# First weight pieces, softmax maxima and reciprocals in PSUM, and v_m products on half rows

## The chip, the cores and the metric

The kernel runs on one core of a Trainium2 chip. The metric is the device time of one execution in microseconds; the median of the runs counts. Engines are named as in the profile: PE is TensorE (matmul), PEld its weight loads, DVE VectorE, ACT ScalarE, POOL GpSimd, SP SyncE (its queue issues the DMAs).

## The reference

Three stages follow one another, all in float32. First a linear attention with 32 memory slots for 8 batches and 8 heads of 576 positions and 64 features; then two feed-forward stages over the 4608 rows of 512 features.

```python
a = softmax(phi, axis=2)                          # over the 576 positions, (8, 8, 576, 32)
k_m = einsum('bhsm,bhsd->bhmd', a, k)             # (8, 8, 32, 64)
v_m = einsum('bhsm,bhsd->bhmd', a, v)
attn = softmax(q @ k_m.T / sqrt(64), axis=-1)     # over the 32 slots
x = attn @ v_m                                    # -> (4608, 512)
h = x @ w_in                                      # (512, 2048)
x = maximum(0.01 * h, h) @ w_out                  # (2048, 512)
out = (sigmoid(x @ w_gate) * (x @ w_val)) @ w2_out
```

The weights arrive in float64, so each element of a weight is two 32-bit words.

## The kernel before, in words

**Precision.** Weights are read as pairs of words and turned into float32 by integer operations (class Piece), and each matrix is then split into a high and a low part (split: a copy on ScalarE, a subtraction on VectorE or GpSimd), so that one product becomes three matmuls.

**Pieces.** The weights of the first feed-forward stage are 32 pieces of 128 x 512 elements, four for each block j of 256 columns of w_in: pieces 4j and 4j+1 are w_in, 4j+2 and 4j+3 rows of w_out. A piece passes five stages: a (three ScalarE passes, L214, L215 and L222: y, k and the sign), b (VectorE, L226, clamps y), b2 (VectorE, L234, shifts y and sets the sign), c (GpSimd, L242, adds k), d (w_out only: the split, at L186 and L187). One call of tick() moves five pieces on by one stage each. The buffers are y (five) and k (four); k comes free when c has run.

**Units.** A unit is one batch and four of its heads. Its parts have names: v1, t1, v2, t2, v3, v3e, v4 are the first softmax (its maximum over positions needs a transpose t1 and a product t2 on TensorE), t4 builds k_m and v_m, v5r and v5x scale them, t5 and v6 transpose them into kvT, t8 and v8 give the scores, v9m, v9s, v9e, v10r, v10m the second softmax, v10t and v11 transpose and split the result. t parts are TensorE's, v parts are others'; upool lists those that GpSimd does.

**Folding v_m into w_in.** Since x = attn @ v_m, the kernel computes vw = v_m @ w_in per batch (vw_block for batch 0, vw_pair for two blocks of a later batch) and then h = attn @ vw in m1_in. For batch 0 kvT holds v_m with zeros in the other half's rows, and vw_block multiplies all 128 rows; vw_pair uses 64 rows for each of the two groups of heads, in two PSUM banks.

**PSUM.** There are eight banks: ps_acc has four (sums of m1_out), ps_h two (m1_in), ps_a two (everything else: t1, t2, t4, t5, t8 and the vw products).

**Order.** All is written out by hand. The prologue computes units 0 and 1 in groups of parts from SCHED; within a group the chains of all units, of the ticks (T) and of a waiting vw split take turns, each up to its next yield. Then 256 steps (batch, half, fc) follow. Step i, in emission order: the split of step i+1's m1_in (gh on ScalarE; gl on GpSimd, or on VectorE for the steps in gldve), then m1_in of step i+2 (six matmuls; gr on ScalarE), the v parts of this step with the held split of the last vw block and the ticks, the t parts, a vw block if the step is in vw0, and m1_out of step i (twelve matmuls). Every engine runs its instructions in this order. A unit's parts stand at fixed distances from its first step (chain1 for batch 1; its units begin at steps 1 and 13). Batch 0's sums are closed after every four steps and copied or added to SBUF (L844 on ScalarE, L842 on VectorE). The second feed-forward stage (m2_group, m2_out) comes after all steps.

## Time and profile before

| | us |
|---|---|
| median of 3 runs | 1602.17 (1600.76 to 8618.76) |
| the profiled execution | 1601.75 |
| its span | 1599.90 |
| TensorE busy in the span | 1549.1 (97%) |
| VectorE busy | 827.7 (52%) |
| ScalarE busy | 707.9 (44%) |
| GpSimd busy | 431.0 (27%) |

The span is the time from the first to the last instruction; the profiled execution's own time lies 1.85 us above it. The page's granted clock is in shares of TensorE's full clock of 2.4 GHz; 0.50 is the lower level of 1.2 GHz. It is at full over the whole span but for the first 80 us and a few short stretches. Most of batch 0 lies between 50 and 160 us, and before 50 us there is the prologue.

### The profile page before, as it was taken

The page shows a single profiled execution, that of the slowest core. Times are in us where ns is not written, and L with a number is a line of the kernel's source. Part 1 is how long each engine was busy: PE and PEld are TensorE (multiplying, and loading weights), DVE is VectorE, ACT ScalarE, POOL GpSimd, SP SyncE. Part 2 cuts the span into 40 slices and gives each one's busy share as a digit, 9 for nine tenths or more (in the row PEclk, how much of TensorE's full clock was granted, in tenths as well). Part 3 has the DMA queues.
Part 4 walks back from the last instruction along what each step waited for, and adds up shares of the span by engine and source line. Part 5 has one row for each costly group of instructions (what it writes and reads, how often), then busy time and mean ns, then how long its engine had stood idle before and what let it go on. Part 6 is the DMA issues. An engine that isn't in the chain of part 4 may idle for free.

```text
span 1599.9 us, 27447 instructions
## 1 busy us (share of the span) xinstructions
PE 1549.1 (97%) x10544; PEld 1358.0 (85%) x10544; DVE 827.7 (52%) x1426; ACT 707.9 (44%) x1602; POOL 431.0 (27%) x429
## 2 busy tenths in 40 slices
PE   5799999999999999999999999999999999999998
PEld 2677988999999998999988888888888888888898
DVE  6886444555554545422145474355545475255544
ACT  5885455565556555645333143223333143223332
POOL 3886343554445444543100020000200020000100
PEclk8799999999999999999999999999999999999999
DMA  9822554554556455322446446536546446536692
GB/s 306 277 53 64 160 143 138 150 154 139 159 146 192 140 160 146 115 82 97 146 170 218 140 156 234 191 115 222 195 163 222 141 150 236 169 109 223 223 398 76
DMA packets 203490, 268.66 MB, mean 168 GB/s; under 512 B 95072, under 2 KB 140128, under 8 KB 203360
## 3 DMA queue, kind: packets, MB, share of 16 engines
q1 hardware_dynamic: 203360, 266.92, 52.1%
q8 instruction: 83, 1.36, 0.4%
q14 instruction: 47, 0.39, 0.1%
HBM read 219.68 MB, written 47.19 MB: 167 GB/s over the span
## 4 chain that ended last, share of the span: by engine, by line
PE 82%; ACT 1%; DVE 1%; DMA 1%; issue 0%; POOL 0%; DVEq 0%; SPq 0%; ACTq 0%; POOLq 0%
PE acc L835 20%; PE oacc L1041 18%; PE ps_y L943 14%; PE ps_h L813 9%; PE ps_x L943 9%; PE ps_z L943 9%; PE ps_vw L783 1%; PE ps_kv L550 1%; DMA wt<-gvs 1%; PE ps_sc L625 0%; ACT gr L818 0%; ACT obuf L844 0%; DVE vw L795 0%; DVE t L530 0%; ACT raw L222 0%
## 5 line engine op out<-in xcount | busy, mean ns | idle before, releaser
L835 PE MATMUL acc<-gh,wo 128*128 128x288 f32 x2048 | 428.7, 301 | 3.7 <-ACT obuf L844 2.7
L835 PEld LDWEIGHTS acc<-gh,wo 128*128 128x128 f32 x2048 | 328.9, 189 | 28.4 <-issue 13.8
L835 PE MATMUL acc<-gl,wo 128*128 128x288 f32 x1024 | 304.8, 298 | 2.1 <-POOL gl L187 2.1
L187 POOL TENSOR_TENSOR gl<-gr,gh 128x288 fp32r<-128x288 f32 x250 | 215.6, 864 | 329.9 <-ACT gh L186 216.6
L1041 PE MATMUL oacc<-w2t,pt 128*128 128x512 f32 x1296 | 296.3, 389 | 0.0
L1041 PEld LDWEIGHTS oacc<-w2t,pt 128*128 128x128 f32 x1296 | 243.1, 188 | 50.3
L943 PE MATMUL ps_y<-xo,wt 128*128 128x512 f32 (+1 forms) x1080 | 251.9, 369 | 0.0
L813 PE MATMUL ps_h<-at_hi,vw 128*128 128x288 f32 x1024 | 214.6, 298 | 6.1 <-ACT vw L186 4.7
L943 PEld LDWEIGHTS ps_y<-xo,wt 128*128 128x128 f32 x1080 | 190.4, 188 | 33.8
L818 ACT ACTIVATE gr<-ps_h 128x288 f32<-128x288 f32 x256 | 105.7, 413 | 254.2 <-PE ps_h L813 226.1
L906 POOL TENSOR_TENSOR xo<-xr,xo 128x512 fp32r<-128x512 f32 (+1 forms) x16 | 23.0, 1460 | 671.0 <-ACT xo L902 671.0
L835 PEld LDWEIGHTS acc<-gl,wo 128*128 128x128 f32 x1024 | 193.7, 189 | 3.0 <-POOL gl L187 3.0
L813 PEld LDWEIGHTS ps_h<-at_hi,vw 128*128 128x128 f32 x1024 | 166.6, 190 | 7.5 <-ACT vw L186 5.6
L943 PE MATMUL ps_z<-xo,wt 128*128 128x512 f32 (+1 forms) x720 | 167.4, 368 | 0.6 <-DMA wt<-gvs 0.6
L943 PE MATMUL ps_x<-xo,wt 128*128 128x512 f32 (+1 forms) x720 | 167.5, 368 | 0.0
L813 PE MATMUL ps_h<-at_lo,vw 128*128 128x288 f32 x512 | 151.6, 296 | 0.0
L978 ACT CAST pt<-sg 128x512 fp32r<-128x512 f32 (+1 forms) x120 | 69.4, 578 | 182.0 <-DVE sg L971 182.0
L943 PEld LDWEIGHTS ps_z<-xo,wt 128*128 128x128 f32 x720 | 127.0, 189 | 23.1 <-DVE tmp L1024 0.7
L943 PEld LDWEIGHTS ps_x<-xo,wt 128*128 128x128 f32 x720 | 127.2, 188 | 22.9
L186 ACT CAST gh<-gr 128x288 fp32r<-128x288 f32 x256 | 111.8, 437 | 2.2
L813 PEld LDWEIGHTS ps_h<-at_lo,vw 128*128 128x128 f32 x512 | 97.2, 190 | 0.0
L990 ACT COPY tmp<-ps_x 128x512 f32<-128x512 f32 (+1 forms) x60 | 32.5, 542 | 136.6 <-PE ps_x L943 136.6
(171 smaller groups left out, 1719.0 us busy)
## 6 DMA issues: line engine op xcount, KB each, us to landing
wt<-gvs SPq DMA_DIRECT2D x210, 512.0 KB, 4.6
w2t<-w2s SPq DMA_DIRECT2D x60, 512.0 KB, 5.5
gvs<-hl SPq DMA_DIRECT2D x84, 256.0 KB, 2.4
x2s<-obuf SPq DMA_DIRECT2D x15, 576.0 KB, 3.7
win<-in_moe_w_in_dram SPq DMA_DIRECT2D x16, 512.0 KB, 9.8
wo_bits<-in_moe_w_out_dram SPq DMA_DIRECT2D x16, 512.0 KB, 10.4
xr<-x2s SPq DMA_DIRECT2D x16, 512.0 KB, 6.2
out_dram<-osum SPq DMA_DIRECT2D x32, 256.0 KB, 2.0
```

What stands on the lines that cost most here:

```text
L186: nc.scalar.copy(hi, raw)
L187: eng.tensor_sub(lo, raw, f32(hi))
L550: nc.tensor.matmul(p[M * h:M * h + M, 0:2 * D], a, x, start=(c == 0), stop=(c == CC))
L783: nc.tensor.matmul(ps[g][M * h:M * h + M, n * VB:(n + 1) * VB], kvT[b, g][D * g:D * g + D, 1, M * h:M * h + M], win[j][D * g:D * g + D, h, ...
L813: nc.tensor.matmul(p[:, :HALF], w, x, start=(n == 0), stop=(n == 3 * NG - 1))
L818: nc.scalar.activation(gr, p[:, :HALF], AF.Prelu, alpha=0.01)
L835: nc.tensor.matmul(a[d][:, :HALF], w[:, ds_], x, start=(open_ and n == 0), stop=(close and n == 2),)
L906: eng.tensor_sub(t[:, 1, :h], x_operand(n, k, a), f32(t[:, 0, :h]))
L943: nc.tensor.matmul(bank, w[:, l, a, :], x[:, r, :h], start=(start and i == 0), stop=(i == 5), skip_group_check=not start,)
L978: nc.scalar.copy(d[:, 0, :h], s)
L990: read(lambda: nc.scalar.copy(s1, x))
L1041: nc.tensor.matmul(bank[i], pt[2 * f + t][:, l, q * P:(q + 1) * P], w2t[f][:, r, :], start=(f == 0 and l + r == 0), stop=(f == TH - 1 and ...
```

## The change

Five things are changed, with the schedule numbers that belong to them:

- The first nine pieces (banks: 9) get their y in a bank of ps_acc from stage a on; b clamps it there, and b2 reads it from there and writes its result to an SBUF y tile.
- In batch 0 the tile st of the second softmax (maximum, sum, reciprocal) lies in a bank of ps_h. GpSimd has no part in v9s and v10m of batch 0 any longer (upool), so VectorE does both.
- The product of the mask and the reciprocal in v5r (VectorE, L565) becomes an activation on ScalarE in v5x, into a tile of its own.
- vw_block makes its products on 64 rows for each group, as vw_pair does, and so takes two tiles of ps_a where it took one; its split is two copies of 256 columns and two subtractions, with a yield between. Blocks 0 and 1 are computed together at the end of the last but one prologue group (W), and their split takes turns with that of the last group.
- v1 of the first unit of batch 1 leaves the prologue. In chain1 v1, t1, v2 and t2 stand at -1, 0, 1 and 2 in place of -5, -1, 0 and 1; block 5 of batch 0 is made at step 12 in place of 13.

```diff
--- before.py
+++ after.py
@@ -18,16 +18,17 @@
 
 
 
-SCHED = {'vw0': [2, 5, 8, 13, 20, 22],
+SCHED = {'vw0': [2, 5, 8, 12, 20, 22],
  'loads': ['p0', 'q0', 'k0', 1, 'p1', 1, 'k1', 'q1', 2, 'p2', 16, 'k2', 32, 'q2.0', 'q2.1', 'q2.2', 'q2.3'],
  'prologue': ['v1.0', 't1.0', 'v2.0 t7a.0 t2.0', 'v7a.0 v3.0', 'v3e.0 v4.0', 't7b.0 v1.1', 'T t4.0 t1.1', 'T',
               'v5.0', 'v7b.0', 'v2.1', 't5.0', 'v6.0 t2.1 t8a.0', 'T v3.1', 'v3e.1 v8a.0 t8b.0', 't7a.1', 'v8b.0',
-              'v9.0 v7a.1 T v4.1 v9e.0 t4.1', 't7b.1 T', 't5.1 v5.1 v7b.1', 'T v1.2', 'v10.0 T', 't8a.1 v6.1',
-              'v10t.0 t8b.1 T v8a.1', 'v11.0', 'v8b.1 v9.1 T', 'T T v9e.1 T v10.1 v10t.1 v11.1'],
+              'v9.0 v7a.1 T v4.1 v9e.0 t4.1', 't7b.1 T', 't5.1 v5.1 v7b.1', 'T', 'v10.0 T', 't8a.1 v6.1',
+              'v10t.0 t8b.1 T v8a.1', 'v11.0', 'v8b.1 v9.1 T', 'T T v9e.1 W', 'T v10.1 v10t.1 v11.1'],
  'ticks': [1, 1, 1, 1, 2, 1, 1, 2, 0, 1, 0, 1, 1, 2, 0, 0, 0, 1, 1, 1, 1, 1, 0, 0, 1, 0, 0, 0, 0, 0],
+ 'banks': 9,
  'lopool': [0, 1, 2, 3, 4, 5, 6, 7, 8, 9, 10, 11, 12, 13, 14],
  'gldve': [3, 4, 6, 12, 26, 31],
- 'upool': ['v10.1', 'v10.2', 'v10.3', 'v11.0', 'v11.1', 'v11.2', 'v11.3', 'v9.0', 'v9.2', 'v9.3'],
+ 'upool': ['v10.2', 'v10.3', 'v11.0', 'v11.1', 'v11.2', 'v11.3', 'v9.2', 'v9.3'],
  'chain': {'lp': -8,
            'lk': -5,
            'lq0': -8,
@@ -94,10 +95,10 @@
             'lq1': 0,
             'lq2': 1,
             'lq3': 2,
-            'v1': -5,
-            't1': -1,
-            'v2': 0,
-            't2': 1,
+            'v1': -1,
+            't1': 0,
+            'v2': 1,
+            't2': 2,
             'v3': 3,
             'v3e': 3,
             'v4': 4,
@@ -195,7 +196,7 @@
     PC = 512
 
     class Piece:
-        late = False
+        late = bank = False
 
         def __init__(self, src, done, f_dst=None, raw=None):
             self.src, self.done, self.f_dst, self.raw = src, done, f_dst, raw
@@ -209,7 +210,10 @@
 
         def a(self):
             w = self.raw.rearrange("p (n t) -> p n t", t=2)
-            self.y = cvp.tile([P, PC], F32, tag="y", name="y", bufs=5)
+            if self.bank:
+                self.y = ps_acc.tile([P, PC], F32, tag="acc", name="y_bank")
+            else:
+                self.y = cvp.tile([P, PC], F32, tag="y", name="y", bufs=5)
             self.k = cvp.tile([P, PC], F32, tag="k", name="k", bufs=4)
             nc.scalar.activation(self.y, w[:, :, 1].bitcast(F32), AF.Abs, scale=2.0 ** -3)
             nc.scalar.activation(self.k, w[:, :, 0], AF.Copy, scale=2.0 ** -27, bias=2.0 ** 25)
@@ -230,9 +234,11 @@
 
         def b2(self):
             w = self.raw.rearrange("p (n t) -> p n t", t=2)
-            yi = self.y.bitcast(I32)
+            y = self.y
+            if self.bank:
+                self.y = cvp.tile([P, PC], F32, tag="y", name="y", bufs=5)
             nc.vector.scalar_tensor_tensor(
-                out=yi, in0=yi, scalar=3, in1=w[:, :, 1].bitcast(I32),
+                out=self.y.bitcast(I32), in0=y.bitcast(I32), scalar=3, in1=w[:, :, 1].bitcast(I32),
                 op0=ALU.logical_shift_left, op1=ALU.bitwise_xor,
             )
             yield
@@ -561,13 +567,13 @@
         yield
         nc.vector.reciprocal(r[:, 0:1], r[:, 0:1])
         yield
+
+    def v5x(u):
+        s = un[u]
+        p, r = s.pop("p"), s["r"]
         if u[0] == 0:
-            nc.vector.tensor_scalar_mul(r, mask, r[:, 0:1])
-            yield
-
-    def v5x(u):
-        s = un[u]
-        p, r = s.pop("p"), s["r"]
+            r = ap_.tile([P, 4], F32, tag="r", name="r", bufs=2)
+            nc.scalar.activation(r, mask, AF.Copy, scale=s["r"][:, 0:1])
         x = etile(u)
         x = s["x"] = x.rearrange("p a m -> p (a m)")[:, 0:4 * D].rearrange("p (a f) -> p a f", a=2)
         if u[0] == 0:
@@ -676,7 +682,10 @@
     def v9m(u):
         s = un[u]
         nb = S // 32
-        st = s["st"] = ap_.tile([P, nb], F32, tag="st", name="st", bufs=2)
+        if u[0] == 0:
+            st = s["st"] = ps_h.tile([P, 512], F32, tag="h", name="st_bank")[:, :nb]
+        else:
+            st = s["st"] = ap_.tile([P, nb], F32, tag="st", name="st", bufs=2)
         nc.vector.reduce_max(st, s["sc"], axis=AX.X)
         yield
 
@@ -757,25 +766,7 @@
             PARTS[n + "ab"[i]] = lambda u, f=f, i=i: f(u, i)
 
 
-    def vw_block(j):
-        p = psa("ps_vw")
-        for g in range(NG):
-            for h in range(HG):
-                nc.tensor.matmul(
-                    p[M * h:M * h + M, g * VB:(g + 1) * VB],
-                    kvT[0, g][:, 1, M * h:M * h + M], win[j][:, h, :], start=True, stop=True,
-                )
-
-        def done():
-            t = vw[0, j] = wtile("vw", [P, 2, NG, VB], F32R, "vw")
-            split(p.rearrange("p (g f) -> p g f", g=NG), t[:, 0], t[:, 1])
-            yield
-
-        return done
-
-
-    def vw_pair(b, j0):
-        js = (j0, j0 + 1)
+    def vw_products(b, js):
         ps = [psa("ps_vw") for _ in range(NG)]
         for n, j in enumerate(js):
             for h in range(HG):
@@ -785,14 +776,39 @@
                         kvT[b, g][D * g:D * g + D, 1, M * h:M * h + M],
                         win[j][D * g:D * g + D, h, :], start=True, stop=True,
                     )
+        return ps
+
+    def vw_split(part, b, js, ps, gs):
+        for g in gs:
+            for n, j in js:
+                x, w = ps[g][:, n * VB:(n + 1) * VB], vw[b, j]
+                if part == "hi":
+                    nc.scalar.copy(w[:, 0, g], x)
+                else:
+                    nc.vector.tensor_sub(w[:, 1, g], x, f32(w[:, 0, g]))
+
+    def vw_tiles(b, js):
         for j in js:
             vw[b, j] = wtile("vw", [P, 2, NG, VB], F32R, "vw")
+
+    def vw_block(j):
+        ps = vw_products(0, (j,))
+
+        def done():
+            vw_tiles(0, (j,))
+            for part in ("hi", "lo"):
+                vw_split(part, 0, [(0, j)], ps, range(NG))
+                yield
+
+        return done
+
+    def vw_pair(b, j0):
+        js = (j0, j0 + 1)
+        ps = vw_products(b, js)
+        vw_tiles(b, js)
         for g in range(NG):
-            ws = [(ps[g][:, n * VB:(n + 1) * VB], vw[b, j]) for n, j in enumerate(js)]
-            for x, w in ws:
-                nc.scalar.copy(w[:, 0, g], x)
-            for x, w in ws:
-                nc.vector.tensor_sub(w[:, 1, g], x, f32(w[:, 0, g]))
+            for part in ("hi", "lo"):
+                vw_split(part, b, list(enumerate(js)), ps, (g,))
 
     hps = {}
     gt = {}
@@ -1099,6 +1115,8 @@
         for j in range(NVB):
             pieces += win_pieces(j) + wout_pieces(j)
         n_start = len(pieces)
+        for p in pieces[:SCHED["banks"]]:
+            p.bank = True
 
         raws = iter(pieces)
 
@@ -1176,6 +1194,19 @@
         def first_vw(j):
             done_until(4 * j + 2)
             return vw_block(j)
+
+        def first_vws():
+            done_until(6)
+            ps = vw_products(0, (0, 1))
+
+            def done():
+                vw_tiles(0, (0, 1))
+                for j in (0, 1):
+                    for part in ("hi", "lo"):
+                        vw_split(part, 0, [(j, j)], ps, range(NG))
+                        yield
+
+            return done
 
         def unit_parts(i):
             vs, ts_, ls = [], [], []
@@ -1199,7 +1230,6 @@
             else:
                 (unit_phi, unit_kv, unit_q)["pkq".index(x[0])](units[int(x[1])])
         waiting = []
-        n_vw = n_in = 0
         fin = None
         for group in SCHED["prologue"]:
             vs, ts_ = {}, []
@@ -1223,12 +1253,7 @@
                 if t:
                     t[0](t[1])
                 else:
-                    waiting.append(first_vw(n_vw))
-                    n_vw += 1
-        run([f() for f in waiting])
-        while n_vw < 2:
-            run([first_vw(n_vw)()])
-            n_vw += 1
+                    waiting.append(first_vws())
         for i in range(LA):
             fin = step_in(*steps[i])
             if i + 1 < LA:
```

## Rows read from the trace of the kernel before

**Rows 1.** Windows: busy us of each engine (instructions), granted clock, DMA share.

```profile
core 0: us, PE busy (x) PEld busy (x) DVE busy (x) ACT busy (x) POOL busy (x), PEclk, DMA share, GB/s
28.00:51.00 23.00, 8.17 (x45) 2.69 (x45) 22.83 (x33) 18.38 (x38) 16.55 (x15) 0.58 1.05 381
99.10:128.40 29.30, 26.47 (x237) 22.96 (x237) 27.14 (x41) 22.43 (x48) 29.22 (x24) 1.00 0.09 19
239.40:243.60 4.20, 4.13 (x42) 3.20 (x43) 2.23 (x7) 1.53 (x5) 0.94 (x2) 0.59 0.38 125
160.00:1599.00 1439.00, 1426.71 (x9525) 1259.83 (x9524) 703.98 (x1232) 596.99 (x1363) 324.17 (x336) 1.00 0.52 167
```

**Rows 2.** Groups of instructions of VectorE, 27 to 51.4 us: count, busy, mean ns.

```profile
L226 DVE TENSOR_SCALAR y<-y 128x512 f32<-128x512 f32 x7 | 6.2, 886 | 0.0
L234 DVE SCALAR_TENSOR_TENSOR y<-y,win 128x512 int32<-128x512 int32 x4 | 5.0, 1250 | 0.0
L234 DVE SCALAR_TENSOR_TENSOR y<-y,wo_bits 128x512 int32<-128x512 int32 x4 | 3.7, 929 | 0.0
L715 DVE TENSOR_TENSOR e<-e,st 128x576 f32<-128x576 f32 x1 | 1.8, 1824 | 0.0
L706 DVE TENSOR_SCALAR st<-st 128x18 f32<-128x18 f32 x2 | 1.2, 622 | 0.1
L479 DVE TENSOR_REDUCE t<-ph 128x128 f32<-128x512 f32 x1 | 1.0, 1032 | 0.0
...
L187 DVE TENSOR_TENSOR vw<-ps_vw,vw 128x512 fp32r<-128x512 f32 x1 | 0.7, 678 | 0.0
```

**Rows 3.** Timeline of VectorE: start, us, line, output and inputs.

```profile
45.68 0.69 DVE L706 TENSOR_SCALAR st<-st 128x18 f32<-128x18 f32 x1
...
97.21 1.65 DVE L842 TENSOR_TENSOR obuf<-acc,obuf 128x288 f32<-128x288 f32 x4 [2.87 <-PE acc L835]
```

**Rows 4.** Timeline of GpSimd, the same columns.

```profile
45.06 1.27 POOL L242 TENSOR_TENSOR y<-y,k 128x512 int32<-128x512 int32 x1 [0.97 <-DVE y L234]
...
96.98 1.29 POOL L242 TENSOR_TENSOR win<-y,k 128x512 int32<-128x512 int32 x1
```

**Rows 5.** Timeline of TensorE: products of one block, of two blocks waiting, of two.

```profile
61.28 1.19 PE L764 MATMUL ps_vw<-win,kvT 128*32 128x256 f32 x16
...
239.47 1.50 PE L783 MATMUL ps_vw<-win,kvT 64*32 64x256 f32 x30 [3.08 <-DVE mx L492]
...
247.25 1.09 PE L783 MATMUL ps_vw<-win,kvT 64*32 64x256 f32 x32
```

**Rows 6.** Chain of waits: start, us, one m1_out of twelve products each.

```profile
240.97 2.92 PE acc L835 x12
244.90 1.62 PE acc L835 x12
```

**Rows 7.** Timeline of VectorE: the gl of step 3.

```profile
63.04 1.30 DVE L187 TENSOR_TENSOR gl<-gr,gh 128x288 fp32r<-128x288 f32 x1 [0.18 <-ACT gh L186]
```

**Rows 8.** Timeline of ScalarE: the scaling L580 at steps 8 and 20.

```profile
90.16 0.47 ACT L580 ACTIVATE e<-ps_kv,r 128x256 f32<-128x256 f32 x1 [1.14 <-DVE r L562]
...
130.15 0.45 ACT L580 ACTIVATE e<-ps_kv,r 128x256 f32<-128x256 f32 x1
```

**Rows 9.** Timeline of TensorE: products of step 8, transposes of steps 9 and 21, step 12.

```profile
85.46 1.53 PE L764 MATMUL ps_vw<-win,kvT 128*32 128x256 f32 x16
...
90.69 0.44 PE L595 MATMUL ps_kvT<-ident,e 128*128 128x128 f32 x2 [0.52 <-ACT e L580]
...
99.45 0.51 PE L835 MATMUL acc<-gh,wo 128*128 128x288 f32 x2
...
103.02 1.06 PE L764 MATMUL ps_vw<-win,kvT 128*32 128x256 f32 x12 [0.37 <-POOL win L242]
...
130.66 0.44 PE L595 MATMUL ps_kvT<-ident,e 128*128 128x128 f32 x2 [0.87 <-ACT e L580]
```

**Rows 10.** Waits of TensorE, 52 to 141 us: total, times, longest.

```profile
PE acc L835 <- POOL gl L187: 2.1, 3, 1.1
...
PE ps_sc L625 <- DVE vw L187: 1.2, 1, 1.2
```

More of the change, by code (lines that the diff above doesn't have):

```diff
@@ L563, in v5r @@
         yield
-        if u[0] == 0:
-            nc.vector.tensor_scalar_mul(r, mask, r[:, 0:1])
-            yield
     def v5x(u):
@@ L678, in v9m @@
         nb = S // 32
-        st = s["st"] = ap_.tile([P, nb], F32, tag="st", name="st", bufs=2)
+        if u[0] == 0:
+            st = s["st"] = ps_h.tile([P, 512], F32, tag="h", name="st_bank")[:, :nb]
+        else:
+            st = s["st"] = ap_.tile([P, nb], F32, tag="st", name="st", bufs=2)
         nc.vector.reduce_max(st, s["sc"], axis=AX.X)
```

## The prediction

> **What bounds the kernel now.** I read the page's 40 slices first: TensorE is busy in nearly all of them, except in the first three, where its granted clock is low as well. So I cut the start and the middle into stretches. From 160 us to the end TensorE works 1426.71 of 1439.00 us at clock 1.00 [rows 1]; nothing that the change edits runs there, so that part only shifts. What can move the total is when the first batch is done, at about 140 us. In 28 to 51 us VectorE is the bound (22.83 of 23.00 us busy, TensorE 8.17); in 99 to 128 us GpSimd is (29.22 of 29.30 us) [rows 1], with TensorE a little behind. The reader is to see two different stages: one in which the change takes work off the bounding engine, and one in which it changes what TensorE waits for.
>
> **Part 1: the first pieces, maxima and reciprocals in PSUM.** In 27 to 51.4 us VectorE's seven first passes (L226) take 6.2 us and its eight second passes (L234) 5.0 + 3.7 us, on average far more than a pass that reads one operand in PSUM, 0.678 us [rows 2]. The excess is waiting for GpSimd: the 18-element add at 45.68 lasts 0.69 us and ends at 46.37, when GpSimd's pass from 45.06, 1.27 us long, has ended at 46.33. Four adds with an operand in PSUM at 97.21 take 0.41 us each while GpSimd is in a pass from 96.98 to 98.27 [rows 3, 4]. So I price every pass that gets a PSUM operand at 0.68 us without waiting.
> VectorE's sum: second passes 8.7 to 8 x 0.68 = 5.4, -3.3. First passes: six of the seven are banked, 6 x 0.68 plus one at 0.89 = 5.0, -1.2. The product L715 1.8 to 0.76 (0.678 scaled from 512 to 576 elements, an estimate), -1.1. The two short adds L706 1.2, taken to lose 0.9 (ends 0 and 1.2). The mask product L565 goes to ScalarE, between two of its instructions, and is counted at nothing on either side. The maximum of the second batch's first unit, L479, 1.0, goes to step 0, where VectorE otherwise waits for ScalarE. Added: two passes that GpSimd did, 2 x 0.76. Together -6.0 us [rows 2].
> ScalarE does not follow that far. It is busy 18.38 of 23.00 us there [rows 1], so at most 4.6 us of waiting can go; the mask product, split copies and the wait for a k buffer that GpSimd frees (four k tiles, as before) keep about 0.9 of that. Taken: -3.7; ends -1.5 (VectorE gains only what leaves it) and -4.6. Writing y to PSUM from ScalarE has no row; I cost it as now, since what it could save is ScalarE time that the k wait covers.
>
> **Part 2: half-row products need both banks of ps_a.** vw_block took one tile of ps_a before and now takes both, and ps_a has two. At each step with such a block (2, 8, 12, 20, 22) TensorE must wait until every other ps_a tile is read; m1_out of that step is queued behind it, and the next ps_a user must wait for the block's own split. The trace shows the price in a block pair of a later batch, which already runs on half rows: 32 products cost 1.09 us at 247.25, but at 239.47 they waited 3.08 us for a maximum on VectorE (L492) [rows 5]; the clock after that wait averaged 0.59 until 243.6 [rows 1], and the m1_out behind it took 2.92 us instead of 1.62 [rows 6].
> The Trainium skill's page "TensorEngine Tiling (Array Packing)" speaks both ways: its section Theoretical Speedup allows up to 2x for 64 contraction rows, its Restrictions and Gotchas warn that row tiles must go to different PSUM banks. The trace agrees with both: 1.09 us for two blocks against 1.19 us for one at 61.28, and the 3.08 us wait. By the first section alone the first rival below comes out, by the second my forecast.
>
> Steps 2 and 3: v2 is moved from step 1 to step 2, so its maximum stands on VectorE behind the gl of step 3, at 63.04 for 1.30 us [rows 7]; with the maximum it ends at 64.6. TensorE would reach the products at 61.0 (61.28 now), so it stands 3.6 us, and is cold after it. Products 1.0, m1_out 2.9 and m1_in 1.1 then end at 69.6; m1_out(2) now follows the products by 62.5, so m1_in(5) now ends at 65 (62.5 + 1.62 + 0.8), and ScalarE's next gr, which needs it, still has about one us of other work then; after the change that gr, and the copies of the group's end behind it, are 3 to 4 us late. **+2.6**, ends +1.1 (warm, 4.6 - 1.9 of cold work - the slack) and +3.0.
> Steps 8 and 9: the second unit's maximum no longer stands between L560 and L562 on VectorE, so L580 (90.16 now, after a wait of 1.14 us for VectorE [rows 8]) comes 1.1 earlier: **-1.1**. But the products, at 85.46 now, need the bank that L580 reads. TensorE stands about 5 us. Now t5 at 90.69 and m1_out(9) follow L580 at once [rows 9]; after the change products, m1_out(8), m1_in(11), then gr, a hi and a lo of the split come between (as t5 needs one of the two banks; 1.2 us is what the present step 23 waits for such a split [rows 10]): 0.55 + 1.62 + 0.8 + 1.2 = 4.2 warm, 6.1 cold. **+5.8**, since 5 us is more than the 3.08 that cooled it.
> Steps 12 and 13: the block is moved from step 13 to 12, ahead of m1_out(12). Its second half needs a piece that GpSimd frees only for 103.02, where m1_out(12) now begins at 99.45 [rows 9]. That pass keeps its place in GpSimd's queue, so m1_out(12) waits until 103.3, +3.9. Step 13 then saves its products, 2.0 us with their wait (102.0 to 104.0), and t1 there waits some 1.1 for the split: +3.0, of which I leave 0.5 to GpSimd being less behind by then. **+2.5** warm, +4.2 cold. Against it, TensorE's three waits for gl on GpSimd, 2.1 us, are used up [rows 10]: **-2.1**.
> Steps 20 to 23: again products behind L580 (130.15 [rows 8]), with t5 now at 130.66 directly after it [rows 9]; +4.2 for what comes between, less 1.1 as TensorE is late itself: **+3.1** (cold +4.4). Step 22's block saves about **-0.5** net.
> The moves of v1 and t1 and the two-part split cost nothing by themselves: they stand where their engine waits. The DMA orders are unchanged, and the queue is not moved past.
>
> **Sum.** -3.7 + 2.6 - 1.1 + 5.8 + 2.5 - 2.1 + 3.1 - 0.5 = +6.6 us. The profiled execution took 1601.75 us (span 1599.90 and 1.85 around it), 0.42 below the median of 1602.17; predicted 1601.75 + 6.6 = **1608.4 us**. All low ends (-4.6 + 1.1 - 1.1 + 4.2 + 2.5 - 2.1 + 3.1 - 0.5) give +2.6, 1604.4; all high ends (-1.5 + 3.0 - 1.1 + 6.1 + 4.2 - 2.1 + 4.4 - 0.5) give +12.5, 1614.3.
>
> **Rivals.** (a) *Faster*: the bank waits are hidden. Then the start's -3.7 and L479's -1.1 stay and the products halve: six blocks of 1.1 to 1.5 us at half, about 4, of which perhaps 1.5 lies on TensorE's path. 1601.75 - 6.3 = 1595.5. For it: from step 3 to 20 ScalarE, VectorE and GpSimd are near full, so TensorE's standing may be time that it would have waited anyway; against it, t5 now follows L580 with nothing between, so whatever is put there is on the path. It decides if L580 at step 8 ends before TensorE has done m1_in(10). (b) *Nothing*: TensorE waits at 2, 8 and 20 but warm, and later waits for GpSimd shrink by as much: -3.7 + 1.1 - 1.1 + 4.2 and no more, about 1602. (c) *Not what it says*: passes with PSUM operands still wait for GpSimd; the start gains 0 and the bank waits stay, +10.3, 1612. Against it stand the adds at 97.21.
>
> **Chances.** Forecast (1604 to 1614) 0.60; (a) 0.22; (b) 0.13; (c) 0.05. The range 1597 to 1613 holds the forecast nearly whole, (b), (c) at its lower part and the upper third of (a), about 0.8. A measurement here can tell about 2%, 32 us, from no change; no case reaches that, so within 2% gets 0.985.
>
> **What would show it.** Right: first passes L226 of pieces 0 to 8 all near 0.68 us; the first m1_in complete 3 to 4 us earlier; the half-row products showing waits of 3 us or more for L492 at step 2, for L580 at steps 8 and 20 and for a GpSimd piece at step 12, with a granted clock of about 0.5 behind them; step 23 some 7 us later than now, and the rest shifted by that. Wrong: those waits under 1 us, or L226 stretched as before. What would upset the sum most is TensorE staying warm through the waits, or GpSimd catching up while TensorE stands.

## The result, and the profile after

The median went from 1601.74 to 1616.38 us (four runs each, the changed kernel's from 1613.33 to 1619.40): ratio 1.0093 [1.0068, 1.0119]. One of the four runs of the kernel before took 8618.76 us, and the ratio leaves it out. The kernel became slower by about 15 us, beyond the upper end of my range; the sign was right, the size was not. The profiled execution took 1615.26 us, its span 1613.50 (before: 1601.75 and 1599.90), so it shows 13.5 of the 14.6 us.

The windows of the changed kernel, with the columns of [rows 1], tell where not to look and where to look:

```profile
core 0: us, PE busy (x) PEld busy (x) DVE busy (x) ACT busy (x) POOL busy (x), PEclk, DMA share, GB/s
28.00:51.00 23.00, 11.53 (x57) 4.88 (x58) 20.13 (x42) 19.42 (x42) 16.40 (x15) 1.00 1.05 386
62.00:66.00 4.00, 4.00 (x28) 3.21 (x29) 1.84 (x3) 1.47 (x4) 3.55 (x4) 0.57 1.05 399
89.50:94.00 4.50, 4.38 (x32) 3.57 (x32) 1.07 (x1) 0.39 (x2) 1.18 (x1) 0.63 0.41 62
99.10:128.40 29.30, 22.36 (x152) 19.51 (x152) 14.95 (x32) 17.20 (x39) 20.46 (x19) 0.88 0.01 3
141.00:146.00 5.00, 4.94 (x30) 4.13 (x31) 1.30 (x1) 0.84 (x3) 3.17 (x3) 0.50 0.78 197
160.00:1599.00 1439.00, 1431.24 (x9652) 1265.69 (x9651) 710.28 (x1245) 604.56 (x1384) 331.94 (x345) 1.00 0.52 167
```

In 28 to 51 us VectorE is no longer full (20.13 us of 23, before 22.83). In 99.1 to 128.4 us, where GpSimd was the bound in [rows 1], it now works 20.46 us of 29.30 and TensorE 22.36: all four engines have idle time there, so somebody waits for somebody in turn. From 160 us on TensorE is busy for 1431.24 us against 1426.71, and the stretch holds 127 more matmuls: that is the tail of the first batch, pushed across 160 us, and not slower work. The three stretches of 4 to 5 us at a granted clock of 0.50 to 0.63 are new (the kernel before has 1.00 in all three): TensorE at the lower of its two levels (1.2 instead of 2.4 GHz) for all or most of them, each time right behind a wait. Two shorter ones lie inside 99.1 to 128.4 us: 0.50 in 109.9 to 113.3 and 0.51 in 123.5 to 127.0.

One figure in that table must not be taken at its word: the granted clock of 1.00 in 28 to 51 us. TensorE's timeline of the changed kernel has there:

```profile
38.29 1.10 PE L774 MATMUL ps_vw<-win,kvT 64*32 64x256 f32 x14 [0.56 <-DVE unit_a L677]
```

Fourteen half-row products take 1.10 us here, as they do below where the clock is low (at 89.62), and 0.66 us where it is full (in an experiment below, at 106.74). So TensorE ran at the lower level here too, whatever the column says.

The plainest measure of the loss is when each step begins its twelve m1_out products (L835 before, L851 after), read off TensorE's timelines of the two profiled executions. (Eight kernels of this document have the changed kernel's prologue, and their step 0 lies between -2.19 and -3.48 us, so one execution's shift is good to about 1 us.)

| step | before, us | after, us | shift |
|---|---|---|---|
| 0 | 56.09 | 53.73 | -2.36 |
| 2 | 62.40 | 62.90 | +0.50 |
| 3 | 64.90 | 68.17 | +3.27 |
| 5 | 76.47 | 74.83 | -1.64 |
| 7 | 82.89 | 81.59 | -1.30 |
| 8 | 87.53 | 90.66 | +3.13 |
| 11 | 96.50 | 101.41 | +4.91 |
| 12 | 99.45 | 109.46 | +10.01 |
| 13 | 104.01 | 114.95 | +10.94 |
| 17 | 115.30 | 128.94 | +13.64 |
| 19 | 122.68 | 135.25 | +12.57 |
| 21 | 130.85 | 148.25 | +17.40 |
| 23 | 140.42 | 157.19 | +16.77 |
| end of span | 1599.90 | 1613.50 | +13.60 |

TensorE's timeline of the changed kernel, columns as in [rows 5] and [rows 9], has a wait at each jump:

```profile
61.93 1.03 PE L774 MATMUL ps_vw<-win,kvT 64*32 64x256 f32 x14 [1.91 <-DVE mx L498]
...
67.93 0.49 PE L507 MATMUL ps_m<-dg,ones 128*128 128x128 f32 x2 [1.22 <-DVE vw L788]
...
89.62 1.10 PE L774 MATMUL ps_vw<-win,kvT 64*32 64x256 f32 x14 [4.85 <-ACT e L586]
...
95.53 0.44 PE L601 MATMUL ps_kvT<-ident,e 128*128 128x128 f32 x2 [1.28 <-DVE vw L788]
...
105.62 0.63 PE L774 MATMUL ps_vw<-win,kvT 64*32 64x256 f32 x6 [0.64 <-DVE e L641]
108.89 0.64 PE L774 MATMUL ps_vw<-win,kvT 64*32 64x256 f32 x8 [2.65 <-POOL win L248]
...
114.86 0.33 PE L493 MATMUL ps_t<-ident,t 128*128 128x128 f32 x1 [1.22 <-DVE vw L788]
...
141.06 1.10 PE L774 MATMUL ps_vw<-win,kvT 64*32 64x256 f32 x14 [2.58 <-ACT e L586]
...
254.99 1.09 PE L774 MATMUL ps_vw<-win,kvT 64*32 64x256 f32 x30 [1.80 <-DVE mx L498]
```

At step 2 the half-row products stand 1.91 us for the maximum (L498), at step 8 4.85 and at step 20 2.58 us for the scaling L586, each because the second bank of ps_a is still being read (the experiments below show it: with one bank these waits are gone). At step 12 they stand 2.65 us for a GpSimd piece, after two short waits for the transposes L641. Behind each, the next user of ps_a waits 1.2 to 1.3 us for the low parts of the block's split on VectorE (L788: at 67.93, 95.53 and 114.86). The Trainium skill's "TensorEngine Tiling (Array Packing)", Restrictions and Gotchas, says that row tiles go to different PSUM banks and that this raises PSUM pressure; the trace agrees, at 4.85 us for one block.

The start shows what the PSUM operands did. VectorE's groups from 18 to 49.6 us, columns as in [rows 2]:

```profile
L230 DVE TENSOR_SCALAR y_bank<-y_bank 128x512 f32<-128x512 f32 x9 | 6.2, 689 | 0.3 <-ACT y_bank L218 0.3
L240 DVE SCALAR_TENSOR_TENSOR y<-y_bank,win 128x512 int32<-128x512 int32 x5 | 3.4, 679 | 0.0
L240 DVE SCALAR_TENSOR_TENSOR y<-y_bank,wo_bits 128x512 int32<-128x512 int32 x4 | 2.7, 682 | 0.0
...
L715 DVE TENSOR_SCALAR st_bank<-st_bank 128x18 f32<-128x18 f32 x2 | 0.4, 176 | 0.0
```

Nine first passes at 0.689 us and nine second passes at 0.68, where [rows 2] had means of 0.886, 1.250 and 0.929 in a slightly later window (in 18 to 49.6 us: 0.773, 1.101 and 0.929); the 18-element adds fell from 0.622 to 0.176 us. The timelines say why, VectorE's first and then GpSimd's:

```profile
40.79 0.69 DVE L230 TENSOR_SCALAR y_bank<-y_bank 128x512 f32<-128x512 f32 x1
41.40 0.68 DVE L240 SCALAR_TENSOR_TENSOR y<-y_bank,wo_bits 128x512 int32<-128x512 int32 x1
...
105.77 0.41 DVE L230 TENSOR_SCALAR y<-y 128x512 f32<-128x512 f32 x1
106.10 0.67 DVE L240 SCALAR_TENSOR_TENSOR y<-y,wo_bits 128x512 int32<-128x512 int32 x1
106.70 0.41 DVE L230 TENSOR_SCALAR y<-y 128x512 f32<-128x512 f32 x1
107.04 0.67 DVE L240 SCALAR_TENSOR_TENSOR y<-y,wo_bits 128x512 int32<-128x512 int32 x1
...
114.38 0.76 DVE L788 TENSOR_TENSOR vw<-ps_vw,vw 128x256 fp32r<-128x256 f32 x2 [6.00 <-ACT vw L786]
```

```profile
40.78 1.28 POOL L188 TENSOR_TENSOR wo<-y,wo 128x512 fp32r<-128x512 f32 x1
...
105.64 3.19 POOL L248 TENSOR_TENSOR win<-y,k 128x512 int32<-128x512 int32 x1
...
116.96 1.29 POOL L188 TENSOR_TENSOR wo<-y,wo 128x512 fp32r<-128x512 f32 x1 [3.25 <-issue]
```

At 40.79 and 41.40 us VectorE's passes on y_bank run 0.69 and 0.68 us inside GpSimd's pass of 40.78 to 42.06: neither waits. At 105.64 the opposite: GpSimd's pass, about 1.27 us when nothing holds it up, lasts 3.19, while VectorE runs four passes with all operands in SBUF (105.77 to 107.71). It ends 1.12 us after the last of them, so it in effect ran behind all four. TensorE's 2.65 us wait at step 12 ends with it. The kernel before has such a pass too, beside the same four passes of VectorE, only later, where no products wait for it:

```profile
118.80 3.21 POOL L242 TENSOR_TENSOR win<-y,k 128x512 int32<-128x512 int32 x1
```

ScalarE's timeline, at step 8, shows the other half of the loss:

```profile
89.09 0.47 ACT L586 ACTIVATE e<-ps_kv,r 128x256 f32<-128x256 f32 x1 [0.28 <-DVE r L568]
...
94.35 0.41 ACT L834 ACTIVATE gr<-ps_h 128x288 f32<-128x288 f32 x1 [4.46 <-PE ps_h L829]
```

After L586, and one copy that follows it, ScalarE stands 4.46 us for m1_in, which is queued on TensorE behind the products that waited for L586. VectorE stands 6.00 us before 114.38, for a copy that ScalarE makes behind another such wait for m1_in (3.24 us, to 113.68). GpSimd stands 3.25 us before 116.96; the profile names no releaser there, but the copy that its pass reads, ScalarE's L187, ended only at 116.83. While TensorE waits, and then works at the lower level, the helpers run dry; at step 15 TensorE waits for them (0.79 us for gh, 1.30 for gl).

### The profile page after: what moved, and what is told of

It reads as the page before. It is cut to its first block, busy times and chain, and to the rows that moved or that the text cites. A ratio compares the mean times of both kernels' runs of the same rounds, so it can differ in the third digit from the quotient of the medians.

```text
span 1613.5 us, 27468 instructions
## 1 busy us (share of the span) xinstructions
PE 1554.9 (96%) x10544; PEld 1362.0 (84%) x10544; DVE 812.4 (50%) x1434; ACT 709.0 (44%) x1612; POOL 425.3 (26%) x427
## 4 chain that ended last, share of the span: by engine, by line
PE 81%; ACT 1%; DVE 1%; DMA 1%; issue 0%; POOL 0%; DVEq 0%; SPq 0%; ACTq 0%; POOLq 0%
PE acc L851 19%; PE oacc L1057 18%; PE ps_y L959 14%; PE ps_h L829 9%; PE ps_x L959 9%; PE ps_z L959 9%; PE ps_vw L774 1%; PE ps_kv L556 1%; DMA wt<-gvs 1%; PE ps_sc L631 0%; ACT gr L834 0%; ACT obuf L860 0%; DVE vw L788 0%; DVE t L536 0%; ACT raw L226 0%
## 5 line engine op out<-in xcount | busy, mean ns | idle before, releaser
L851 PE MATMUL acc<-gh,wo 128*128 128x288 f32 x2048 | 431.6, 303 | 1.0 <-ACT gh L187 0.8
L851 PEld LDWEIGHTS acc<-gh,wo 128*128 128x128 f32 x2048 | 331.7, 191 | 26.0 <-issue 14.6
L851 PE MATMUL acc<-gl,wo 128*128 128x288 f32 x1024 | 306.2, 299 | 1.4 <-POOL gl L188 1.3
L851 PEld LDWEIGHTS acc<-gl,wo 128*128 128x128 f32 x1024 | 195.3, 191 | 1.9 <-POOL gl L188 1.9
L959 PEld LDWEIGHTS ps_z<-xo,wt 128*128 128x128 f32 x720 | 127.0, 189 | 23.3 <-DVE tmp L1040 0.9
L187 ACT CAST gh<-gr 128x288 fp32r<-128x288 f32 x256 | 111.9, 437 | 2.2
L788 DVE TENSOR_TENSOR vw<-ps_vw,vw 128x256 fp32r<-128x256 f32 x128 | 45.8, 418 | 117.0 <-ACT vw L786 116.9
```

The lines of the kernel that those rows point to most:

```text
L187: nc.scalar.copy(hi, raw)
L788: nc.vector.tensor_sub(w[:, 1, g], x, f32(w[:, 0, g]))
L851: nc.tensor.matmul(a[d][:, :HALF], w[:, ds_], x, start=(open_ and n == 0), stop=(close and n == 2),)
L959: nc.tensor.matmul(bank, w[:, l, a, :], x[:, r, :h], start=(start and i == 0), stop=(i == 5), skip_group_check=not start,)
```

## The experiments

All were timed in five rounds beside the kernel before (its medians: 1601.15 us for the first four, 1601.63 for the next four, 1601.25 for the last four). "Step 23" is the shift of the start of m1_out(23) against the kernel before (140.42 us).

**One bank (the changed kernel, blocks 2 to 7 as before on all rows in one bank, new places kept).**

```diff
     def vw_block(j):
-        ps = vw_products(0, (j,))
+        p = psa("ps_vw")
+        for g in range(NG):
+            for h in range(HG):
+                nc.tensor.matmul(
+                    p[M * h:M * h + M, g * VB:(g + 1) * VB],
+                    kvT[0, g][:, 1, M * h:M * h + M], win[j][:, h, :], start=True, stop=True,
+                )
...
```

> The changed kernel, but the blocks 2 to 7 of batch 0 multiply all 128 rows into one bank of ps_a, as before the change; the new schedule (block 5 at step 12, v1 to t2 later) and all that lies in PSUM stay. Theory A (the second ps_a bank makes TensorE wait): the waits for L498 at step 2 and L586 at steps 8 and 20 go; the wait for the GpSimd piece at step 12 stays, about 3 us; m1_out(23) comes 14 us or more earlier than in the changed kernel, time 1599 to 1603 us. Theory B (the moved parts and the block at step 12 cost): time stays at 1612 or more. Theory C (passes in PSUM and the softmax passes that VectorE took over slow the first batch): 1612 or more, first m1_out no different and VectorE late in steps 0 to 8.

Measured 1605.59 us, ratio 1.0027 [1.0017, 1.0037]; step 23 +4.25. The two banks are worth some 11 us (1616.38 to 1605.59; 12.5 at step 23). The shift is still -3.47 at step 11 and becomes +3.34 at step 12 and +7.77 at step 17: what is left comes from there. TensorE's timeline, then GpSimd's, of this kernel:

```profile
100.95 1.91 PE L798 MATMUL ps_vw<-win,kvT 128*32 128x256 f32 x12 [4.29 <-POOL win L248]
```

```profile
97.72 3.18 POOL L248 TENSOR_TENSOR win<-y,k 128x512 int32<-128x512 int32 x1
```

Block 5 at step 12 waits 4.29 us for the stretched GpSimd pass even with one bank.

**Two banks, all 128 rows (the changed kernel; only the rows differ).**

```diff
-                        kvT[b, g][D * g:D * g + D, 1, M * h:M * h + M],
-                        win[j][D * g:D * g + D, h, :], start=True, stop=True,
+                        kvT[b, g][r, 1, M * h:M * h + M],
+                        win[j][r, h, :], start=True, stop=True,
```

with r all 128 rows for blocks 2 to 7.

> The changed kernel, but the blocks 2 to 7 multiply all 128 rows while still taking two banks. Theory A: the same waits as in the changed kernel, and up to 0.5 us more for each of six blocks: 1616 to 1620 us. If the half rows themselves (the short products, the two row halves at a time) caused the loss, the time falls below 1608.

Measured 1618.81 us, 1.0113 [1.0099, 1.0126]; step 23 +14.92. TensorE's timeline at steps 2 and 8, and the window behind step 2:

```profile
61.67 1.09 PE L775 MATMUL ps_vw<-win,kvT 128*32 128x256 f32 x14 [2.17 <-DVE mx L498]
...
88.25 1.78 PE L775 MATMUL ps_vw<-win,kvT 128*32 128x256 f32 x14 [4.77 <-ACT e L586]
```

```profile
62.00:66.00 4.00, 3.32 (x32) 2.61 (x24) 1.58 (x3) 1.86 (x6) 3.54 (x4) 1.00 1.05 400
```

The waits stay (2.17 and 4.77 us), so they belong to the banks and not to the half rows. The half rows by themselves save: 14 products take 1.09 us at clock 1.00 here, where half rows at full clock take 0.66 (below, at 106.74). The two kernels' intervals overlap, so that saving does not show in the time.

**Blocks 4 and 6 elsewhere (the changed kernel).**

```diff
-SCHED = {'vw0': [2, 5, 8, 12, 20, 22],
+SCHED = {'vw0': [2, 5, 10, 12, 18, 22],
```

> The changed kernel, but block 4 is made at step 10 in place of 8 and block 6 at step 18 in place of 20, where no unscaled ps_kv holds a bank. Theory A: the waits for L586 (4.85 and 2.58 us) and those for the split behind them go, at step 10 a wait under 1 us for L613 comes: 6 to 10 us less than the changed kernel, 1606 to 1610 us. Theory B or C: within 2 us of it, 1614 to 1618.

Measured 1609.36 us, 1.0048 [1.0036, 1.0061]; step 23 +8.09. TensorE's timeline of this kernel:

```profile
94.76 0.66 PE L774 MATMUL ps_vw<-win,kvT 64*32 64x256 f32 x14 [0.49 <-ACT kvT L613]
...
99.27 1.04 PE L631 MATMUL ps_sc<-qT,kvT 64*32 64x288 f32 x16 [1.28 <-DVE vw L788]
```

The wait for L586 is gone (0.49 us for another reader instead); but the score products behind the block still wait 1.28 us for the split. At step 9 the shift is +0.22 instead of +4.85, but the block comes only then: at step 11 it is +3.74 instead of +4.91. The larger gains come later: step 12 adds 2.1 us instead of 5.1, since GpSimd's pass falls elsewhere and takes 1.28 us (at 103.41), and steps 18 to 21, with block 6 two steps earlier, add 0.4 us instead of 3.8. So moving the two blocks saves some 7 us, but not all of it is the wait for L586. Two-bank blocks cost something wherever they stood here.

**The reverse: the kernel before with two-bank half-row blocks 2 to 7 in the new places (late v1 to t2 too), and nothing else of the change.**

```diff
+        def vw_half(j):                      # blocks 2 to 7: vw_products, both banks
...
-            return vw_block(j)
+            return vw_block(j) if j < 2 else vw_half(j)
...
-SCHED = {'vw0': [2, 5, 8, 13, 20, 22],
+SCHED = {'vw0': [2, 5, 8, 12, 20, 22],
```

> The kernel before, with half-row products in two banks for the blocks 2 to 7 and the schedule numbers that they need (block 5 at step 12, v1 to t2 of batch 1 later), blocks 0 and 1 as before; nothing else of the change (y and st in SBUF, GpSimd's softmax passes, the mask product on VectorE). Theory A: m1_out(23) some 17 to 20 us later than in the kernel before, 1615 to 1620 us. Theory C: within 3 us of the kernel before, 1600 to 1605.

Measured 1620.53 us, 1.0129 [1.0115, 1.0143]; step 23 +19.29. This part alone is no faster than the whole change (the intervals just overlap), and the same waits come up at steps 8 and 12:

```profile
92.06 1.10 PE L765 MATMUL ps_vw<-win,kvT 64*32 64x256 f32 x14 [4.75 <-ACT e L580]
...
112.38 1.08 PE L765 MATMUL ps_vw<-win,kvT 64*32 64x256 f32 x8 [2.64 <-POOL win L242]
```

**The start alone (one bank, block 5 back at step 13, v1 to t2 and v1.2 where they were).**

```diff
-SCHED = {'vw0': [2, 5, 8, 12, 20, 22],
+SCHED = {'vw0': [2, 5, 8, 13, 20, 22],
...
-            'v1': -1,
-            't1': 0,
-            'v2': 1,
-            't2': 2,
+            'v1': -5,
+            't1': -1,
+            'v2': 0,
+            't2': 1,
```

> The one-bank kernel of the first experiment with the order of the kernel before as well: block 5 at step 13, v1 to t2 of batch 1 at their old places, v1 of its first unit back in the prologue. What is left of the change is the start: y, st and reciprocals in PSUM, the mask product on ScalarE, blocks 0 and 1 on half rows and their split in turns with the last group. Theory A (all of the loss lies in the two banks and in the order that they force): m1_out(0) and every later step 2 to 4 us earlier than in the kernel before, 1597.5 to 1599.5 us, faster than both kernels. Theory C (PSUM passes cost later): 1602 or more.

Measured 1598.06 us, 0.9978 [0.9969, 0.9987], faster than the kernel before by 3.6 us; step 23 -2.76, step 0 -2.52: the gain of the start is carried through the first batch. (One more us in its trace comes from a block pair of the second batch, steps 56 to 58.) TensorE's timeline of this kernel:

```profile
87.84 0.44 PE L601 MATMUL ps_kvT<-ident,e 128*128 128x128 f32 x2 [0.52 <-ACT e L586]
...
100.18 1.06 PE L798 MATMUL ps_vw<-win,kvT 128*32 128x256 f32 x12 [0.35 <-POOL win L248]
```

t5 stands 0.52 us behind L586 and block 5's products 0.35 us, as in [rows 9].

**The same without y in PSUM** ('banks': 9 to 0; nothing else of the previous kernel).

> As the kernel of e5, but with y of all pieces in SBUF (banks 0). If the first pieces in PSUM make the gain of the start by ending VectorE's waits for GpSimd, m1_out(0) comes 2 us or more later than in e5 and the time is 1600 to 1602 us. If the maxima, the reciprocals and the interleaved split make it, it stays within 0.7 us of e5.

Measured 1600.54 us, 0.9995 [0.9986, 1.0004]; step 0 -0.30 instead of -2.52. VectorE's groups, 18 to 49.6 us:

```profile
L230 DVE TENSOR_SCALAR y<-y 128x512 f32<-128x512 f32 x10 | 6.2, 617 | 0.0
L240 DVE SCALAR_TENSOR_TENSOR y<-y,win 128x512 int32<-128x512 int32 x5 | 5.5, 1108 | 0.0
L240 DVE SCALAR_TENSOR_TENSOR y<-y,wo_bits 128x512 int32<-128x512 int32 x4 | 4.9, 1218 | 0.0
```

The second passes take 1.108 and 1.218 us again instead of 0.68. The first passes are on average no slower without PSUM (0.617 against 0.688): in SBUF they vary from 0.39 to 1.51 us here, in PSUM they all took 0.67 to 0.70. So y in PSUM pays in the second pass, and is worth about 2.2 us at step 0 and 2.5 us of the median.

**The same with the second softmax's maxima and reciprocals in SBUF** (with y in PSUM; st in SBUF, and v9.0 and v10.1 on GpSimd again).

```diff
-        if u[0] == 0:
-            st = s["st"] = ps_h.tile([P, 512], F32, tag="h", name="st_bank")[:, :nb]
-        else:
-            st = s["st"] = ap_.tile([P, nb], F32, tag="st", name="st", bufs=2)
+        st = s["st"] = ap_.tile([P, nb], F32, tag="st", name="st", bufs=2)
```

> As the kernel of e5, but with st of batch 0 in SBUF and GpSimd again doing v9s of unit 0 and v10m of unit 1. If the maxima and reciprocals in PSUM on VectorE are worth anything, m1_out(0) comes 0.7 us or more later than in e5; if they only move 2 passes of 0.75 us to VectorE, it comes earlier. My sum had them at -1.1 - 0.9 + 1.5 on VectorE, so within 1 us either way: 1597 to 1600.5 us.

Measured 1603.12 us (1598.88 to 1603.63), 1.0005 [0.9996, 1.0014]; step 0 -0.85, so this part is worth 1.7 us there, where I had expected about none. Of the rest of its 5 us against the start-alone kernel, 3.1 us lie in one wait of a block pair of the second batch (the two traces are 2.2 us apart at step 56 and 5.3 at step 58). TensorE's timeline of the start-alone kernel, then of this one:

```profile
235.64 1.09 PE L774 MATMUL ps_vw<-win,kvT 64*32 64x256 f32 x30 [2.03 <-DVE mx L498]
```

```profile
240.39 1.95 PE L771 MATMUL ps_vw<-win,kvT 64*32 64x256 f32 x30 [3.91 <-DVE mx L498]
```

A wait of 2.03 us there, of 3.91 here. There the products still run at full clock (1.09 us) and the clock falls only behind them (0.50 in 236.8 to 240.2 us); here it is low already (1.95 us).

**One bank, only block 5 back at step 13** (v1 to t2 late, as in the change): the first experiment with 'vw0': [2, 5, 8, 13, 20, 22].

> The one-bank kernel of the first experiment with block 5 back at step 13, v1 to t2 of batch 1 still late. Theory A with the order as second cause: the wait of 4.3 us for the GpSimd piece at step 12 falls below 0.6; if that makes the whole rest of the loss, 1597.5 to 1599.5 us. If the late t2 of the second unit (wait of 3.1 us for L501 at step 15 in the first experiment) costs by itself, 1600 to 1602.5.

Measured 1598.20 us, 0.9977 [0.9968, 0.9986]; step 23 -2.07. All that the first experiment left open is block 5's place: 7.4 us. The moves of v1 to t2 cost nothing that the time shows. Undone in this order, the medians give 10.8 us for the two banks, 7.4 for block 5's place and -3.4 for the rest, which is the start; at step 23 it is 12.5, 6.3 and -2.1. The third experiment shows that the first two are not independent: moving blocks 4 and 6 took the wait for GpSimd at step 12 away as well.

**Two banks, blocks 4, 5 and 6 at steps 10, 14 and 18** ('vw0': [2, 5, 10, 14, 18, 22] in the changed kernel).

> The changed kernel with two banks and half rows, block 4 at step 10, block 5 at step 14 and block 6 at step 18. Theory A with the early block 5 as second cause: against the third experiment (block 5 at step 12) the waits for L641 and for the split before t1 at step 13 go, and a wait for L498 of the second unit, 1 to 3 us, comes at step 14, behind m1_out(13): 1605 to 1609 us. If step 12 costs only because the piece of GpSimd is late, about 1604 to 1606.

Measured 1611.63 us (1607.73 to 1612.82), 1.0058 [1.0046, 1.007]: not the gain I expected, and not to be told from the third experiment. The profiled execution was one of the faster ones (1608.34 us). Step 13 is at +1.19, as hoped, but step 15 at +6.36, step 18 at +10.47 and step 23 at +7.84. TensorE's timeline of this kernel:

```profile
115.05 0.80 PE L507 MATMUL ps_m<-dg,ones 128*128 128x128 f32 x2 [3.21 <-DVE vw L788]
```

The product t2 of the next unit now waits 3.21 us for the block's split, and block 6 at step 18 waits 2.04 us for a GpSimd pass of 3.19 us. The stops moved, they did not go.

**The forced passes one step earlier** (the changed kernel, ticks of step 11 from 1 to 2 and of step 12 from 1 to 0 in that list, so that VectorE's four passes do not fall on GpSimd's).

> The changed kernel, with one tick moved from step 12 to step 11, so that GpSimd adds the last piece of block 5 one step earlier. If the late piece makes the loss of steps 12 and 13 (+6.0 us there, a wait of 2.65 us and low clock behind it), that wait falls below 0.5 and the time to 1609 to 1612 us. If the banks alone make it (L641 at 12, the split before t1 at 13), 1614 to 1617.

TensorE's timeline of this kernel, then GpSimd's:

```profile
105.51 0.59 PE L774 MATMUL ps_vw<-win,kvT 64*32 64x256 f32 x2 [1.07 <-POOL wo L188]
106.74 0.66 PE L774 MATMUL ps_vw<-win,kvT 64*32 64x256 f32 x14 [0.64 <-DVE e L641]
```

```profile
105.29 1.28 POOL L248 TENSOR_TENSOR win<-y,k 128x512 int32<-128x512 int32 x1
```

GpSimd's pass takes 1.28 instead of 3.19 us, and the products wait 0.64 us for the transposes instead of 2.65 for the pass, but 1.07 us for another GpSimd instruction before them. Steps 12 and 13 add 3.58 us (+5.28 at step 11 to +8.86) instead of 6.03. So the stretched pass was 2.4 us of those 6.0. The median is 1613.63 us (1609.78 to 1620.99), 1.0080 [1.0062, 1.0098]: 2.8 us lower, about as much, but the interval overlaps the changed kernel's, and the time is above the 1609 to 1612 that I expected. The profiled execution was the slowest of the six, 1620.99 us, because it lost 4.5 us more behind step 23, so only its first batch is read here.

**The clock held up** (the changed kernel with 8, 26 and 12 useless matmuls, at_hi by at_hi into a bank of ps_h, ahead of the blocks of steps 2, 8 and 20; they only add work).

```diff
+            if i in {2: 8, 8: 26, 20: 12}:
+                p = ps_h.tile([P, 512], F32, tag="h", name="ps_warm")
+                for _ in range({2: 8, 8: 26, 20: 12}[i]):
+                    nc.tensor.matmul(p[:, :HALF], at_hi[:, 0, 0:P], at_hi[:, 0, :], start=True, stop=True)
```

> The changed kernel, with products of no use ahead of the blocks of steps 2, 8 and 20 (8, 26 and 12 matmuls of 128x288 into a free bank of ps_h, about 1.1, 3.5 and 1.6 us), which fill most of TensorE's waits there. If the low clock behind the waits is a cost of its own, the granted clock stays at 1.00 behind steps 8 and 20, the block and m1_out behind each wait take about 2.3 us in place of 4, and the time falls by 3 to 5 us, to 1611 to 1613. If only the waiting counts, it stays at 1616 or grows.

The windows of this kernel, and its TensorE timeline at step 8 and in the second batch:

```profile
62.00:66.00 4.00, 2.78 (x21) 2.55 (x20) 1.93 (x5) 2.27 (x7) 3.70 (x3) 1.00 1.04 399
89.50:94.00 4.50, 3.22 (x26) 2.98 (x25) 2.62 (x6) 3.47 (x8) 0.18 (x1) 1.00 0.36 58
141.00:146.00 5.00, 4.20 (x37) 3.14 (x38) 3.37 (x6) 1.69 (x6) 2.46 (x2) 1.00 0.40 88
```

```profile
87.22 0.66 PE L774 MATMUL ps_vw<-win,kvT 64*32 64x256 f32 x14 [1.38 <-ACT e L586]
...
251.31 1.96 PE L774 MATMUL ps_vw<-win,kvT 64*32 64x256 f32 x30 [3.90 <-DVE mx L498]
```

The granted clock is 1.00 in all three stretches (after: 0.57, 0.63, 0.50), the products take 0.66 instead of 1.10 us, and step 23 is at +10.31 instead of +16.77; 1.1 us of that stand at step 0 already, before any useless matmul. Yet the median is 1614.49 us, 1.0087 [1.0074, 1.0100]: the intervals overlap, and it is above the 1611 to 1613 that I expected. In its profiled execution 4.3 us of the gain went again behind step 23, at the pair of the second batch, which waited 3.90 us and ran at the lower level (1.80 us and full clock in the changed kernel, at 254.99); its span is 1611.30. The clock behind the waits is shown in the trace, its share of the time is not.

**Start alone with one later pair earlier** ('vw2': [54, 55, 59, 64] for [54, 57, 59, 64], against that wait of the second batch).

> The kernel of e5 (one bank, order of before), with the second block pair of batch 2 made two steps earlier, at step 55 in place of 57, where no maximum is waited for. In every kernel so far TensorE waits there for L498, 1.8 to 3.9 us, sometimes with low clock behind it. Expected: that wait goes, 1594 to 1596.5 us, faster than e5 and both kernels. If the pair's vw tiles come free later than I think, the wait only changes its name and the time stays at 1598.

Measured 1597.36 us, 0.9974 [0.9964, 0.9984]: the lowest median, but not to be told from the start-alone kernel (0.9978), and above the 1594 to 1596.5 that I expected. The wait for L498 went, and a wait of 1.50 us for the pair's split came (t1 at 234.48).

## Why the prediction was wrong

The terms of my sum against the table above. Each measured figure is the difference of two shifts, the last one that from step 23 to the end of the span:

| term | predicted | measured |
|---|---|---|
| start | -3.7 | -2.4 |
| steps 2 and 3 (to step 7) | +2.6 | +1.1 |
| steps 8 and 9 (to step 11) | -1.1 + 5.8 | +6.2 |
| steps 12 and 13 | +2.5 | +6.0 |
| slack on GpSimd (steps 14 to 19) | -2.1 | +1.6 |
| steps 20 and 21 | +3.1 | +4.8 |
| step 22 (to 23) | -0.5 | -0.6 |
| later | 0 | -3.2 |
| sum | +6.6 | +13.6 |

**The steps that failed are steps 12 and 13, and the slack.** Together they are 7.2 us off, all of the 7.0 that are missing; the other errors cancel. That they cancel is luck: at step 23, which I had put some 7 us late, the kernel was 16.77 us late, and 3.2 us came back afterwards for a reason that was not in my sum. For step 12 I took m1_out(12) to wait 3.9 us for a pass that "keeps its place in GpSimd's queue", and kept its length of before too (1.72 us, at 101.25). But the block's place also forces the pieces' passes: VectorE's four unbanked passes now fall on that GpSimd pass and stretch it to 3.19 us (2.4 us of the step, by the run with the forced passes a step earlier). The pass of 3.21 us at 118.80 in the trace of before could have warned me. The clock fell behind that wait, which I allowed for only in the upper end: m1_out(12) took 2.92 us (109.46 to 112.38) and not 1.84. The run with one bank and block 5 at step 13 settles the place: 7.4 us of its time, where I had +2.5.

For the slack I took TensorE's three waits for gl, 2.1 us [rows 10], to be used up, as if GpSimd and ScalarE ran on while TensorE stood. They don't: gr needs m1_in, which TensorE issues in order behind the block. So they stand as well (4.46 us before 94.35, 6.00 before 114.38, 3.25 before 116.96), and have the same work still to do when TensorE starts again. GpSimd's busy time fell from 29.22 to 20.46 us of the same 29.30: not slack gained, but work pushed out of the window. TensorE's waits there did not shrink either: one of 1.3 us for gl and one of 0.8 for gh make 2.1 again, and the clock fell behind them (0.51 in 123.5 to 127.0 us). In the run with the forced passes a step earlier, steps 14 to 19 add 1.6 us again, so this is not the stretched pass. That the standing helpers are the whole reason is read from these rows and not tested by a run of its own.

**Steps 2 and 3** ended lower. The places and the clock were right (wait 1.91 us, not 3.6; granted clock 0.57 in 62 to 66; step 3 at +3.27), but by step 5 TensorE was 1.64 us early again. What came back is a stop that the kernel before has there itself, and that my sum did not hold. TensorE's timeline of the kernel before:

```profile
70.20 0.85 PE L835 MATMUL acc<-gh,wo 128*128 128x288 f32 x2 [2.73 <-ACT obuf L844]
```

It waits 2.73 us for ScalarE's copies of the group's end and runs m1_out(4) cold, 3.25 us from 70.20. After the change ScalarE begins those copies at the same 69.77 us; TensorE, late itself, no longer waits, and m1_out(4) takes 1.75 us. This is not the gain of the start: the old kernel with two-bank blocks, which has no such gain, is at +5.78 at step 3 and at +0.88 at step 5. Here TensorE's lateness did use up a wait, which is what I had assumed, wrongly, of the slack above.

**Steps 8 and 9, and 20 and 21**, were right in mechanism, order and rough size: 6.2 for 4.7, 4.8 for 3.1. Both lie somewhat above the cold ends that I gave (5.0 and 4.4); the clock was 0.63 and 0.50 behind them. The two-bank runs without half rows and in the old kernel show the same waits, the run with blocks 4 and 6 elsewhere is without them.

**The start** was right in kind: passes with a PSUM operand run beside GpSimd at 0.68 to 0.69 us, nine of nine, so rival (c) is out. It gave 2.4 us where I took 3.7, between my ends of 1.5 and 4.6. My account of its parts was off: first passes gain little by PSUM (0.617 us without in one run, 0.773 in the kernel before, 0.688 with), second passes do, and the maxima and reciprocals are worth 1.7 us at step 0 and not the 0.5 of VectorE's time (-1.1 - 0.9 + 1.5) that I booked for them.

**Later**, 3.2 us came back that nothing in my sum held: the pair at 239.47 in [rows 5] waited 3.08 us and ran cold behind it, after the change it waited 1.80 and stayed warm, and 2.8 of the 3.2 us lie at that pair (+16.79 at step 56, +13.97 at step 58). I had taken the rest as only shifted.

Rival (a), faster, lost where I had put its point of decision: L586 at step 8 ends at 89.56 us, 4.8 us after TensorE had reached the products. Rival (b) asked for warm waits and helpers that catch up; but for the copies at step 4, neither came.

What stays open: how much of the 15 us is the clock by itself, since the run that held it up was not measurably faster. Between kernels the single wait in the second batch differs by about 2 us (1.80 to 3.91), and several kernels spread by 5 us and more over their runs; differences of medians below some 3 us between my experiments I don't build on.

## What to carry to other kernels

Before a faster product form takes a second bank of a two-bank pool, list who still reads that pool at each place where it is put: here six blocks that each saved somewhat under half a microsecond of TensorE cost some 11 us. When engines run in order and feed one another, a wait of one need not use up the slack of the others: at step 4 it did, in steps 14 to 19 it did not. Book it only where the row shows that the other engine's work can go on, and price the passes that a moved step forces along with it. Undo the parts of a change one by one: the start alone, mainly its PSUM operands, is 3.6 us faster than the kernel before.

## What was not expected of the hardware

- A GpSimd pass on SBUF waited out four successive VectorE passes: 3.18 to 3.21 us instead of 1.27, in the changed kernel, in the one-bank kernel and, at another place, in the kernel before. The Trainium skill's "SBUF — State Buffer", Who interferes with whom, has the loser blocked for the other's whole instruction; the trace agrees, and shows it for a row of instructions, between which GpSimd did not get its turn.
- Waits of about 2 us are not alike for the clock: after 1.91 us at step 2 the granted clock was 0.57 in 62 to 66 us, after 2.17 us with full-row products 1.00 in the same window.
- The granted-clock column can mislead at the start of a trace. In 28 to 51 us it shows 1.00 for the changed kernel and 0.51 for the start alone, but the same fourteen half-row products take 1.10 us in both (at 38.29 and 38.04). The length of the matmuls decides.
